# Spectral mixing with a gated FFN on one core: background work queued only when its engine is free, loads counted longer, two phases paced anew

## The chip, the core and the metric

The kernel runs on one core of a Trainium2 chip. The core has five engines with a queue each: TensorE (PE, matrix products), VectorE (DVE), ScalarE (ACT), GpSimd (POOL) and SyncE (SP), which here issues nearly all DMA transfers. Each queue is worked off in the order in which the program was written, and an instruction that waits for a semaphore holds up everything behind it on its engine. The metric is device time in microseconds; lower is better. The kernel before takes 1803.35 us, the median of three runs (1802.31 to 1805.86).

## What is computed

The input `x` is 8192 tokens of 448 features. It is normalised per token, and two things are made of the normalised tokens: a spectral mixing (a Fourier transform over tokens and features, a two-layer block-diagonal MLP on the spectrum, a soft threshold, the inverse transform) and a gated feed-forward net whose result goes through a SiLU. The output is `x + s * g`.

```python
def reference(A_x, A_w1, A_b1, A_w2, A_b2, B_x, B_w_gate, B_w_up, B_w_down):
    def _A_ref(x, w1, b1, w2, b2):            # spectral mixing; 4 blocks of 112 features
        Xf = rfft2(x, axes=(1, 2)); z = Xf.reshape(B, H, Wf, NB, BS)
        hr = zr @ w1[0] - zi @ w1[1] + b1[0];  hi = zi @ w1[0] + zr @ w1[1] + b1[1]
        hr, hi = relu(hr), relu(hi)
        or_ = hr @ w2[0] - hi @ w2[1] + b2[0]; oi_ = hi @ w2[0] + hr @ w2[1] + b2[1]
        or_, oi_ = soft_threshold(or_, 0.01), soft_threshold(oi_, 0.01)
        return irfft2(or_ + 1j * oi_)
    def _B_ref(x, w_gate, w_up, w_down):      # 448 -> 1792 -> 448
        return (_gelu(x @ w_gate) * (x @ w_up)) @ w_down
    xn = _layernorm(A_x)
    s = _A_ref(xn, A_w1, A_b1, A_w2, A_b2)
    g = _silu(_B_ref(xn, B_w_gate, B_w_up, B_w_down))
    return A_x + s * g
```

The block above is shortened; `@` stands for the einsum over one block.

## The kernel before

Products are made in 16-bit pairs: a 32-bit operand is split into a high and a low half, and three products stand for one. The low half is always made by a subtraction (`B.tensor_sub`), the high one by an ACT copy.

**Foreground.** `ffn` runs the feed-forward net in chunks of 512 tokens, in two passes over the 14 blocks of 128 hidden features: pass 0 takes blocks 0 to 7, pass 1 blocks 8 to 13 (`PF`). Each pass has 16 chunks. From chunk 2 on, the gate and up products of a pair of blocks are made in seven products in place of eight (`unit`); its operands are sums and differences of the input's quarters, written to DRAM as `xts` by the background and read back by two transposing DMAs (tiles `xta` and `xtb`). The product with `w_down` is made in the plain way (`down`) until the background has set up the tiles `left` and `right`, and from the next chunk on in seven products too (`down2`).

**Background.** It fills the engines between the foreground's instructions.
- Phase one: `chunk1` takes 512 tokens, normalises them (`stats`, `norm`), makes the operands of the seven products (`factors`, tiles `sf` and `sx`), and does the first stage of the transform (`stage1`: product of `xs` with `m`, then `ysb`). Chunk c enters at `T1 + (c - PL) * DT`. Beside it `weights` prepares the weights: for each far block `gu_loads` loads it into `wst`, `gu_block` finds its largest value (`fm`, then `fx` by way of a small product on PE), scales and splits it, `gu_comb` makes its sums; then `down_weights` and `factors0` do the same for `w_down` (the ACT row `wst<-wst,fd` is their scaling), and `prep_mlp` loads the MLP.
- Phase two: `group` runs the MLP on the spectrum, 16 groups of 4 blocks, spread evenly up to `END2`.
- Phase three: `tiles3` does the last stage of the transform and the gating with what pass 1 of the foreground has stored in `gsp` up to that point. Chunks of pass 1 that begin after phase three is opened are gated directly (`state["direct"]`, `gate_bank`, `gate`), without that round trip.

**The order.** All this is written as coroutines, and `Pace` decides at build time in which order their instructions go into the queues. It keeps a clock per engine from rough costs (`Pace.cost`) and always resumes the coroutine whose time is least; a coroutine that yields gives way. A DMA on SP is counted by `Pace.issue`: 0.5 us of the queue, and a landing 2.2 us plus its size over 240 KB/us after its start. `B` (class `Either`) puts a subtraction on DVE or POOL, whichever ends it first by those clocks. Background instructions go in when their coroutine's turn comes, also when their engine's clock stands further on, and the foreground's next instruction then stands behind them.

On the chip nothing of those clocks is left but the order: an instruction waits for its operands, and what is behind it in its queue waits too. All instructions are recorded from one helper, so each row of the profile says L199, and rows are told apart by their tiles.

Of the kernel before, what the change touches and what calls it, by code (L numbers as in the profile page):

```python
# [13 lines left out]
AF = mybir.ActivationFunctionType  # L14
# [7 lines left out]
NG = 16  # L22
# [17 lines left out]
EPS = 1e-5  # L40
LAM = 0.01
# [7 lines left out]
class Pace:  # L49
# [82 lines left out]
    def issue(self, e, op, out, ins, run):  # L132
        outs, ins, start = self.start(e, out, ins)
        if e == "SP":
# [69 lines left out]
class Either:  # L204
# [5 lines left out]
    def __getattr__(self, op):  # L210
# [7 lines left out]
        return call  # L218

# [154 lines left out]
def afno_geglu_kernel(ctx, tc, x, gu, wd, mlp, b1, b2, c_m, c_mt, c_small, out):  # L374
# [81 lines left out]

    EV = {}
# [46 lines left out]
    def stats(c):  # L504
# [26 lines left out]
    def factors(c, q, xs):  # L531
# [8 lines left out]
        B.tensor_sub(sf[:, 1, :], sf[:, 0, :], xn[:, 0, 0:K1])  # L540
        yield
        B.tensor_sub(sf[:, 3, 0:K2], xn[:, 0, K1:], sf[:, 1, 0:K2])
# [3 lines left out]
        yield  # L546
        S.copy(low[:, 0:K2], sf[:, 3, 0:K2])
        B.tensor_sub(big[:, :, 1, :], sf[:, 0:3, :], big[:, :, 0, :])
        yield
        B.tensor_sub(low[:, K2:K1], sf[:, 3, 128:K2], low[:, 128:K2])  # L550
        B.tensor_sub(low[:, K1:], sf[:, 3, 0:128], low[:, 0:128])
# [39 lines left out]
    def chunk1(c):  # L591
# [5 lines left out]
        for q in range(2):  # L597
            xs = yield from XS.get()
            for a in (2 * q, 2 * q + 1):
                norm(c, a)  # L600
                yield
            xn = EV["x4", c][:, 2 * q:2 * q + 2, :]
            f = pace.spawn(factors(c, q, xs))
            S.copy(xs[:, :, 0, :], xn)
            yield
            B.tensor_sub(xs[:, :, 1, :], xn, xs[:, :, 0, :])
# [27 lines left out]
    T1, DT = 84.0, 42.0  # L634
# [27 lines left out]
    def gu_block(b, to):  # L662

        f0, n = BLK[b]
        for i in range(n):
            yield ev("wl", f0 + i, 0)
            t = EV["wst", f0 + i, 0]
            V.tensor_reduce(fm[:, i, :, b], t[:, 0:8].rearrange("p (i k) f -> p i (k f)", i=2),
# [43 lines left out]
    def gu_split(f, t, d, k):  # L712
        if 0 < f < PF[0][1]:
            for i in range(2):
                w = t[:, 4 * i:4 * i + 4]
                S.activation(w, w, AF.Copy, scale=scale(f, i))
                S.copy(d[:, 0, 4 * i:4 * i + 4], w)
            yield
            for i in range(2):
                B.tensor_sub(d[:, 1, 4 * i:4 * i + 4], t[:, 4 * i:4 * i + 4], d[:, 0, 4 * i:4 * i + 4])  # L720
            yield
            return
        S.activation(d[:, 0, 0:4 - k], t[:, k:4], AF.Copy, scale=scale(f, 0))
# [1495 lines left out]
```

## Time and profile before

| | |
|---|---|
| median of three runs | 1803.35 us (1802.31 to 1805.86) |
| the profiled execution | 1803.61 us, its span 1801.8 us |
| PE busy | 1762.4 us, 98% of the span, 16017 matmuls |
| DVE, ACT, POOL busy | 77%, 57%, 28% |
| mean granted clock of TensorE | 0.996 |
| DMA | 285 MB, 158 GB/s over the span |

The span goes from the first to the last instruction; 1.8 us of the execution lie outside it. A row of a timeline gives the start in us, how long the piece took, the engine, the operation with its tiles (out<-in) and how many instructions are merged; in brackets at its end stands how long the engine had been idle before, and what it had waited for. Rows of windows give each engine's busy time in a stretch of the span, the granted clock of TensorE (PEclk, 1.00 is full speed) and the share of the DMA engines.

### The profile page before, as it was taken

Reading aid. Unit: us, or ns where it says so; the run is one execution under the profiler, and the core shown is the slowest. Engines: PE = TensorE matmul, PEld = TensorE weight load, DVE = VectorE, ACT = ScalarE, POOL = GpSimd, SP = SyncE. Lnnn points to the kernel's source line nnn. Section 1 sums busy time; section 2 is a strip of 40 time slices with the busy share of each in tenths; the row PEclk is TensorE's granted clock in tenths of the full one; section 3 lists DMA queues with packets and bytes.
Section 4 is the critical chain, followed back from the end, with each engine's and each line's share of the span. In section 5 each row is a group of like instructions: output and inputs, shape, how many; then the busy total and the mean of one; then the engine's idle time right before and its main releaser. Section 6 shows DMA issues by size and latency. Waiting matters only on the chain. (4 is left out here: it accounts for less than half of the span.)

```text
span 1801.8 us, 39863 instructions
## 1 busy us (share of the span) xinstructions
PE 1762.4 (98%) x16017; PEld 1457.2 (81%) x16017; DVE 1385.6 (77%) x2518; ACT 1021.1 (57%) x1977; POOL 500.7 (28%) x582
## 2 busy tenths in 40 slices
PE   7999999999999999999999999999999999999998
PEld 3447677776777767898999999999999999888887
DVE  7867587777766668767868878888888887788886
ACT  5736365554554444546767666767767774333333
POOL 3332232231322223212313223233333431221211
PEclk9999999999999999999999999999999999999999
DMA  6454665576647753513335634544344435999991
GB/s 218 159 152 126 172 177 165 170 213 172 192 138 201 199 170 98 162 52 80 77 115 165 184 90 120 120 95 109 87 113 122 114 89 153 302 286 301 315 311 53
DMA packets 353866, 285.35 MB, mean 158 GB/s; under 512 B 235184, under 2 KB 323760, under 8 KB 353680
## 3 DMA queue, kind: packets, MB, share of 16 engines
q1 hardware_dynamic: 353392, 282.24, 55.0%
q8 instruction: 125, 2.05, 0.5%
q10 hardware_dynamic: 288, 0.56, 0.1%
q14 instruction: 61, 0.50, 0.1%
HBM read 128.36 MB, written 105.23 MB: 130 GB/s over the span
## 5 line engine op out<-in xcount | busy, mean ns | idle before, releaser
L199 PEld LDWEIGHTS <-wt 128*128 128x128 f16 x9350 | 909.7, 98 | 170.0 <-issue 14.9
L199 PE MATMUL bx<-xta,wt 128*128 128x256 f16 (+1 forms) x3843 | 475.1, 275 | 0.2 <-ACT th L199 0.2
L199 PEld LDWEIGHTS <-h 128*128 128x128 f16 x2708 | 260.0, 98 | 105.0 <-issue 3.4
L199 PE MATMUL bd<-dw,h 128*128 128x448 f16 (+1 forms) x1704 | 282.8, 317 | 2.5 <-DVE pt L199 0.8
L199 PE MATMUL by<-xtb,wt 128*128 128x256 f16 x2080 | 252.9, 273 | 2.4 <-DVE by L199 2.4
L199 PE MATMUL by<-xta,wt 128*128 128x256 f16 (+1 forms) x1347 | 177.2, 281 | 4.2 <-DVE xta L199 3.1
L199 POOL TENSOR_TENSOR wt<-wt 128x256 f32<-128x256 f32 x78 | 61.3, 786 | 286.2 <-DVE wt L199 270.3
L199 PE MATMUL bx<-xtb,wt 128*128 128x256 f16 x1040 | 130.5, 272 | 1.1 <-DVE v L199 0.7
L199 DVE TENSOR_TENSOR by<-bx,u 128x512 f32<-128x512 f32 x104 | 72.5, 697 | 71.8 <-PE bx L199 64.9
L199 ACT COPY u<-by 128x512 f32<-128x512 f32 x104 | 60.8, 584 | 89.9 <-PE by L199 89.0
L199 POOL TENSOR_TENSOR zs<-t,zs 112x256 f16<-112x256 f32 (+2 forms) x50 | 57.0, 1139 | 159.0 <-ACT zs L199 159.0
L199 ACT ACTIVATE u<-by,fc 128x512 f32<-128x512 f32 (+1 forms) x118 | 73.4, 634 | 46.9 <-PE by L199 46.2
L199 PE MATMUL bd<-dw,wt 128*128 128x224 f16 (+1 forms) x816 | 97.7, 264 | 0.9 <-DVE pt L199 0.6
L199 ACT CAST h<-wt 128x512 f16<-128x512 f32 (+1 forms) x128 | 68.4, 535 | 41.4 <-DVE wt L199 35.7
L199 ACT ACTIVATE th<-bd,fb 128x448 f32<-128x448 f32 x62 | 39.0, 634 | 87.5 <-PE bd L199 72.7
L199 PE MATMUL bf<-w2t,wn 112*128 112x112 f16 x1512 | 84.9, 213 | 0.0
L199 ACT COPY by<-bx 128x512 f32<-128x512 f32 x104 | 59.7, 575 | 42.7 <-PE bx L199 42.3
L199 DVE SCALAR_TENSOR_TENSOR pt<-bd,fb,pt 128x448 f32<-128x448 f32 (+1 forms) x97 | 65.3, 676 | 23.6 <-PE bd L199 22.8
L199 DVE TENSOR_TENSOR v<-bx,u 128x512 f32<-128x512 f32 x104 | 71.2, 685 | 15.8 <-PE bx L199 15.1
L199 PEld LDWEIGHTS <-wn 112*128 112x128 f16 x1512 | 80.6, 98 | 1.2
L199 ACT ACTIVATE gl<-bx,fc 128x512 f32<-128x512 f32 (+1 forms) x70 | 40.5, 600 | 71.0 <-PE bx L199 63.6
L199 DVE SCALAR_TENSOR_TENSOR u<-by,fc,u 128x512 f32<-128x512 f32 (+1 forms) x86 | 55.4, 658 | 25.5 <-PE by L199 13.9
(240 smaller groups left out, 3148.1 us busy)
## 6 DMA issues: line engine op xcount, KB each, us to landing
xts<-sx SPq DMA_DIRECT2D x32, 480.0 KB, 3.0
x<-in_x SPq DMA_DIRECT2D x17, 896.0 KB, 6.5
t<-ysb SPq DMA_DIRECT2D x64, 224.0 KB, 3.3
prt<-th SPq DMA_DIRECT2D x64, 224.0 KB, 2.9
pt<-prt SPq DMA_DIRECT2D x64, 224.0 KB, 3.8
u<-t SPq DMA_DIRECT2D x32, 448.0 KB, 6.2
x<-in_x SPq DMA_DIRECT2D x32, 448.0 KB, 7.0
y<-t SPq DMA_DIRECT2D x30, 448.0 KB, 3.8
```

Source lines behind the costliest of these rows:

```text
L199: return self.pace.issue(self.name, kind, out, ins, lambda: fn(out, *args, **kw))
```

## The change

It has four parts.
1. `CALM`: before a background instruction, its coroutine now waits until its engine's clock is not ahead of the present by more than 0.05 us. For ACT and DVE this is `yield from calm(...)` ahead of the instruction; for subtractions that may go to DVE or POOL it is `B.calm`, which takes the one of the two engines that is free, and if none is, waits for the first that will be. Before 200 us of the order's clock (`QUIET`) nothing of this waits. It is put into `stats`, `factors`, `chunk1`, and the weights' functions (`gu_block`, `gu_split`, `gu_comb`, `factors2`, `down_weights`), not into `stage1`, phase two or phase three.
2. A plain load (DMA into on-chip memory) that starts after 100 us is counted as landing 2.5 us later.
3. Chunks of phase one enter every 38 us in place of 42 (`DT`), so that `END1` moves by 64 us, and the gaps between steps of the far weights are 10 us in place of 20.
4. `END2`, up to which phase two is spread, is 1410 in place of 1450.

```diff
+CALM, QUIET = 0.05, 200.0
...
-                end = max(start + 2.2 + size / 240e3, self.dma + 1.5)
+                end = max(start + 2.2 + size / 240e3, self.dma + 1.5) + (2.5 if outs and start > 100.0 else 0.0)
...
+    def calm(self, op, out, *args):
+        pace = self.pace
+        while True:
+            ends = []
+            for e in self.engines:
+                if pace.free.get(e.name, 0.0) <= pace.now + CALM or pace.now < QUIET:
+                    _, _, start = pace.start(e.name, out, args)
+                    ends.append((start + pace.cost(e.name, op, start, out, args), len(ends), e))
+            if ends:
+                return getattr(min(ends)[2], op)(out, *args)
+            yield min(pace.free[e.name] for e in self.engines)
...
+    def calm(e):
+        while pace.free.get(e, 0.0) > pace.now + CALM and pace.now >= QUIET:
+            yield pace.free[e]
...
+        yield from calm("ACT")
         S.copy(sf[:, 0, K2:], xn[:, 1, K2:K1])
-        B.tensor_add(sf[:, 0, 0:K2], xn[:, 1, 0:K2], xn[:, 1, K1:])
-        B.tensor_sub(sf[:, 2, :], xn[:, 0, 0:K1], xn[:, 1, 0:K1])
+        yield from B.calm("tensor_add", sf[:, 0, 0:K2], xn[:, 1, 0:K2], xn[:, 1, K1:])
+        yield from B.calm("tensor_sub", sf[:, 2, :], xn[:, 0, 0:K1], xn[:, 1, 0:K1])
...
-    T1, DT = 84.0, 42.0
+    T1, DT = 84.0, 38.0
...
             t = EV["wst", f0 + i, 0]
+            yield from calm("DVE")
             V.tensor_reduce(fm[:, i, :, b], t[:, 0:8].rearrange("p (i k) f -> p i (k f)", i=2),
...
+            yield from calm("ACT")
             S.activation(v, v, AF.Copy, scale=fd[:, 2, block(f):block(f) + 1])
...
-    END1, END2, END3 = T1 + NG * DT + 12.0, 1450.0, 1765.0
+    END1, END2, END3 = T1 + NG * DT + 12.0, 1410.0, 1765.0
...
-            yield pace.now + 20.0
+            yield pace.now + 10.0
             pace.spawn(gu_loads(range(BLK[b][0], sum(BLK[b])), 0))
             yield pace.spawn(gu_block(b, 1))
```

Three places show what it does to the order. In these rows a row is one instruction or a run of equal ones (x2), with its tiles and the shape it writes.

The first place is the first pair of far blocks. On SP its two loads are `wst<-in_gu 128x1408`; `xta` and `xtb` are the transposing loads of the foreground's next chunk, the `xts` rows store the background's operands, `t<-ysb` the first stage of the transform. Before:

```order
L199 DMA_TRANSPOSE xta<-xts 128x16x256
L199 DMA t<-ysb 64x1792 x2
L199 DMA_TRANSPOSE xtb<-xts 128x9x256
L199 DMA xts<-sx 128x1920
L199 DMA xts<-xs 128x2x256
L199 DMA xts<-xs 128x2x192
L199 DMA xts<-xs 128x2x64
L199 DMA xts<-xs 128x2x128
L199 DMA t<-ysb 64x1792 x2
L199 DMA wst<-in_gu 128x1408 x2
L199 DMA prt<-th 128x448 x3
```

And on SP of the changed kernel:

```order
L200 DMA t<-ysb 64x1792 x2
L200 DMA xts<-sx 128x1920
L200 DMA xts<-xs 128x2x256
L200 DMA xts<-xs 128x2x192
L200 DMA xts<-xs 128x2x64
L200 DMA xts<-xs 128x2x128
L200 DMA t<-ysb 64x1792 x2
L200 DMA wst<-in_gu 128x1408 x2
L200 DMA_TRANSPOSE xta<-xts 128x16x256
L200 DMA_TRANSPOSE xtb<-xts 128x9x256
```

The two loads stood behind both transposes and now stand ahead of them.

On DVE, at the same place, `fm<-wst` reads those loads, `ysb` is the last piece of the first stage of the transform, the `h`, `gl`, `u`, `v` and `by` rows are the foreground's. Before:

```order
L199 SCALAR_TENSOR_TENSOR gl<-v_1951,fc,gl 128x512
L199 SCALAR_TENSOR_TENSOR ysb<-bf,ysb 128x2x224
L199 TENSOR_TENSOR h<-gl,h 128x2x256
L199 SCALAR_TENSOR_TENSOR ysb<-bf,ysb 128x2x224
L199 TENSOR_REDUCE fm<-wst 128x2 x2
L199 BN_STATS st<-x_1668 128x6
L199 BN_AGGR st<-st 128x2
L199 TENSOR_TENSOR fx<-fm 128x2
```

And on DVE of the changed kernel:

```order
L200 SCALAR_TENSOR_TENSOR ysb<-bf,ysb 128x2x224
L200 TENSOR_TENSOR by<-bx,u_1927 128x512
L200 SCALAR_TENSOR_TENSOR gl<-v_1886,fc,gl 128x512
L200 SCALAR_TENSOR_TENSOR u_1975<-by,fc,u_1975 128x512
L200 TENSOR_TENSOR h<-gl,h 128x2x256
L200 TENSOR_TENSOR v_2001<-bx,u_1927 128x512
L200 TENSOR_TENSOR h<-u_1975,h 128x2x256
L200 SCALAR_TENSOR_TENSOR gl<-v_2001,fc,gl 128x512
L200 BN_STATS st<-x_1563 128x6
L200 BN_AGGR st<-st 128x2
L200 TENSOR_REDUCE fm<-wst 128x2
```

The reduction stood right behind the last `ysb`, and now seven instructions of the foreground and the first statistics stand between them.

The second place is on ACT, at the first `wst<-wst,fd`, which scales the first loaded piece of `w_down`; `xs` is the high half of the background's tokens, from which PE makes the first stage of the transform, and `th` the foreground's output of a chunk. Before:

```order
L199 ACTIVATE th<-bd,fb 128x448 x2
L199 ACTIVATE wst<-wst,fd 128x896
L199 CAST xs<-x_4145 128x2x448
L199 COPY sf<-x_4145 128x64
L199 ACTIVATE th<-bd,fb 128x448
L199 CAST sx<-sf 128x3x256
```

And on ACT of the changed kernel:

```order
L200 ACTIVATE th<-bd,fb 128x448 x2
L200 CAST xs<-x_4344 128x2x448
L200 ACTIVATE th<-bd,fb 128x448
L200 COPY sf<-x_4344 128x64
L200 ACTIVATE wst<-wst,fd 128x896
L200 ACTIVATE ysb<-bf 128x2x224
```

The scaling, which waits for a load, stood ahead of `xs` and now stands behind it.

The third place is on POOL, in a chunk of phase one, from the square roots of its statistics (`st`) on. Before:

```order
L199 TENSOR_TENSOR st<-st 128x4
L199 TENSOR_TENSOR xs<-x_3179,xs 128x2x448
L199 TENSOR_TENSOR sf<-x_3179,sf 128x192
L199 TENSOR_TENSOR sx<-sf,sx 128x3x256
L199 TENSOR_TENSOR h<-gl,h 128x2x256
L199 TENSOR_TENSOR sx<-sf,sx 128x64
L199 TENSOR_TENSOR h<-u_3825,h 128x2x256
```

And on POOL of the changed kernel:

```order
L200 TENSOR_TENSOR st<-st 128x4
L200 TENSOR_TENSOR xs<-x_2525,xs 128x2x448
L200 TENSOR_TENSOR sf<-x_2525 128x192
L200 TENSOR_TENSOR sf<-x_2525 128x256
L200 TENSOR_TENSOR sf<-sf,x_2525 128x256
L200 TENSOR_TENSOR sf<-x_2525,sf 128x192
L200 TENSOR_TENSOR sx<-sf,sx 128x3x256
L200 TENSOR_TENSOR sx<-sf,sx 128x64
L200 TENSOR_TENSOR sx<-sf,sx 128x128
```

POOL did a part of the operands, mixed with subtractions of the foreground's `h`; now it does the whole chain of them in a row. Over the program POOL has 644 instructions where it had 587, and DVE 2463 where it had 2520; ACT has the same number. PE has the same products except for one chunk of pass 1 that is now gated directly (chunks 9 to 14 are gated directly, where 10 to 14 were; the last chunk goes its own way in both): 24 products of 224 columns for 12 of 448. The chunk from which the down product is made in seven products is the same, chunk 12 of pass 0.

More of the change, by code (lines that the diff above doesn't have):

```diff
@@ L599, in chunk1 @@
             for a in (2 * q, 2 * q + 1):
+                yield from calm("DVE")
                 norm(c, a)
@@ L667, in gu_block @@
             t = EV["wst", f0 + i, 0]
+            yield from calm("DVE")
             V.tensor_reduce(fm[:, i, :, b], t[:, 0:8].rearrange("p (i k) f -> p i (k f)", i=2),
@@ L746, in gu_comb @@
             yield ev("spare", f - 2 if f < 6 else f)
+        yield from calm("ACT")
         S.activation(d[:, 0], c, AF.Copy, scale=scale(f, 0))
         yield
+        yield from calm("DVE")
         V.scalar_tensor_tensor(d[:, 1], c, scale(f, 0), d[:, 0], op0=ALU.mult, op1=ALU.subtract)
@@ L757, in factors2 @@
         if block(f) == block(f + 1):
+            yield from calm("ACT")
             S.activation(v, v, AF.Copy, scale=fd[:, 2, block(f):block(f) + 1])
@@ L760, in factors2 @@
             for e in range(2):
+                yield from calm("ACT")
                 S.activation(v[:, e], v[:, e], AF.Copy, scale=fd[:, 2, block(f + e):block(f + e) + 1])
@@ L821, in most @@
             for i in range(n):
+                yield from calm("DVE")
                 V.tensor_reduce(dmx[:, f + i:f + i + 1], v[:, i], axis=AXIS.X, op=ALU.max, apply_absolute_value=True)
```

53 lines of the change are left out of this document (30 added, 23 removed).

## The prediction

> **What bounds the kernel now.** I read the page's engine rows first, then the same by stage, then who waited for whom, then the timeline at the waits that PE ends up with.
>
> ```profile
> span 1801.8 us, 39863 instructions
> PE 1762.4 (98%) x16017; PEld 1457.2 (81%) x16017; DVE 1385.6 (77%) x2518; ACT 1021.1 (57%) x1977; POOL 500.7 (28%) x582
> ...
> 0.00:45.00 45.00, 31.62 (x166) 16.97 (x167) 34.31 (x87) 24.38 (x54) 14.23 (x22) 0.96 0.62 218
> 45.00:90.00 45.00, 41.95 (x213) 19.40 (x212) 39.04 (x83) 32.77 (x61) 13.74 (x14) 1.00 0.50 159
> ...
> 45.00:800.00 755.00, 742.42 (x5528) 536.50 (x5527) 539.97 (x1024) 394.54 (x722) 211.67 (x292) 1.00 0.56 161
> 800.00:1500.00 700.00, 696.67 (x7638) 644.14 (x7637) 568.44 (x1014) 489.79 (x1004) 213.44 (x200) 1.00 0.44 112
> 1500.00:1700.00 200.00, 199.00 (x1838) 177.05 (x1836) 165.13 (x267) 76.50 (x135) 41.70 (x47) 1.00 0.90 280
> 1700.00:1802.00 102.00, 92.67 (x857) 82.53 (x854) 77.78 (x129) 35.85 (x64) 19.66 (x22) 0.98 0.62 195
> ```
>
> The first number after a stretch's length is PE's busy time. PE is the bound in every stage: of 1801.8 us it is idle 39.4. Of these 13.4 lie before 45 us, 3.1 in 45:90 and 9.3 after 1700, most of them filling and draining. What a better order can win is the rest: 12.6 - 3.1 = 9.5 us in 90:800, 3.3 in 800:1500, 1.0 in 1500:1700, together 13.8 us, and what a slowed clock costs beside it.
>
> The waits say where it comes from.
>
> ```profile
> PE bf L199 <- DVE fx L199: 6.3, 2, 3.8
> PE bf L199 <- DVE k L199: 2.5, 4, 1.0
> PE by L199 <- DVE by L199: 2.4, 3, 1.7
> PE bd L199 <- DVE h L199: 0.7, 2, 0.5
> ...
> DVE fm L199 <- DMA wst<-in_gu: 17.8, 4, 14.4
> ...
> ACT wst L199 <- DMA wst<-in_down: 8.2, 3, 3.7
> ```
>
> PE never waits for a transfer itself, but DVE does, for the far blocks' weights, 17.8 us in 4 waits, and ACT, for `w_down`, 8.2 us in 3 (total, times, longest). Both are background instructions, ahead of the foreground's in their queues. The timelines of SP, DVE and PE at the longest of them, with the windows around it:
>
> ```profile
> 196.80 4.12 SPq L199 DMA_TRANSPOSE xtb<-xts  x1
> ...
> 205.29 1.51 SPq L199 DMA_DIRECT2D wst<-in_gu  x2
> ...
> 211.93 1.22 DVE L199 TENSOR_REDUCE fm<-wst 128x2 f32<-128x1024 f32 x1 [14.45 <-DMA wst<-in_gu]
> 214.10 1.22 DVE L199 TENSOR_REDUCE fm<-wst 128x2 f32<-128x1024 f32 x1 [0.95 <-DMA wst<-in_gu]
> ...
> 204.78 5.08 PE L199 MATMUL bd<-dw,h 128*128 128x448 f16 x26
> 209.70 1.47 PE L199 MATMUL bx<-xta,wt 128*128 128x256 f16 x12
> 211.01 1.47 PE L199 MATMUL by<-xta,wt 128*128 128x256 f16 x12
> 216.27 0.59 PE L199 MATMUL bf<-identf,fx 128*2 128x128 f32 x2 [3.79 <-DVE fx L199]
> 216.79 2.74 PE L199 MATMUL bx<-xta,wt 128*128 128x256 f16 x12
> ...
> 215.00:222.00 7.00, 5.73 (x27) 3.76 (x28) 5.06 (x17) 1.41 (x3) 2.06 (x6) 0.52 0.39 155
> ```
>
> The load goes out at 205.29 and lands 6.6 us later, DVE sits 14.45 us on its reduction, and PE has the small product `fx` in its queue and stands still for 3.79 us. After that the granted clock is 0.52 over 7 us: the same twelve products take 2.74 us where they took 1.47. The other places, on ACT, DVE and PE:
>
> ```profile
> 437.59 1.04 ACT L199 ACTIVATE wst<-wst,fd 128x896 f32<-128x896 f32 x1 [3.72 <-DMA wst<-in_down]
> ...
> 439.51 0.35 PE L199 MATMUL bf<-xs,m 128*128 128x448 f16 x1 [0.64 <-ACT xs L199]
> 440.72 0.54 PE L199 MATMUL bf<-xs,m 128*128 128x448 f16 x2 [0.85 <-DVE xs L199]
> ...
> 458.19 1.04 ACT L199 ACTIVATE wst<-wst,fd 128x896 f32<-128x896 f32 x1 [3.60 <-DMA wst<-in_down]
> ...
> 461.64 1.25 PE L199 MATMUL by<-xtb,wt 128*128 128x256 f16 x10 [1.74 <-DVE by L199]
> ...
> 285.78 1.22 DVE L199 TENSOR_REDUCE fm<-wst 128x2 f32<-128x1024 f32 x1 [1.91 <-DMA wst<-in_gu]
> ...
> 287.65 1.25 PE L199 MATMUL by<-xtb,wt 128*128 128x256 f16 x10 [0.31 <-DVE by L199]
> ```
>
> **The change, part by part.** *Loads counted 2.5 us longer.* The old count, 2.2 us plus size over 240 KB/us, gives 5.2 us for a load of 704 KB and 4.1 for 448 KB. What they took, issue to landing:
>
> ```profile
> wst<-in_gu SPq DMA_DIRECT2D x14, 704.0 KB, 6.0
> ...
> wst<-in_down SPq DMA_DIRECT2D x10, 448.0 KB, 5.5
> ```
>
> With 2.5 more the count is 7.7 and 6.6, above both medians, and above the 6.6 of the load at 205.29. So the waits of this kind should shrink by 2.5 us each, and those on the path are of 1.91, 3.72 and 3.60; the 14.45 is a matter of the queue's order.
>
> Term 1, the far block at 212: 3.79 us of idle PE, and half the clock after it. From 215 to 222 a share of 0.48 of the clock is missing, of which the first 1.27 us are idle anyway: (7 - 1.27) x 0.48 = 2.75. Together 6.5 us. Would it be gone? The loads now stand on SP ahead of the two transposes, of which `xtb` alone held SP for 4.12 us. On PE there stand, between the last product of the transform's first stage and `fx`, 64 products of 256 columns and 60 of 448 where there were 24 and 72. By the starts above (209.70 to 211.01 for 12, 204.78 to 209.70 for 26) these take 0.109 and 0.189 us each: 18.3 us now, 16.2 before. Needed are some 3 us for the last `ysb` and the stores ahead of the load (an estimate: twice the 1.51 us that issuing two transfers took), 8.8 until both loads are there (205.29 to 214.10), 1.2 for the second reduction: 13 us of 18. I take all 6.5.
>
> Term 2, the two waits for `w_down`: 0.64 + 0.85 + 1.74 = 3.2 us of PE. At the first, `xs` now stands ahead of the scaling, so that a late load holds up nothing PE waits for; at the second the 3.60 falls to about 1.1, less than the 3.60 - 1.74 = 1.9 that PE had in reserve. All 3.2 gone.
>
> Term 3, at 287: 0.31.
>
> *Background only into a free engine.* An instruction that waits no longer for a turn behind others costs the same engine time, it comes later. The foreground's short waits that are left in 90:800 are 9.5 - 3.8 - 3.2 - 0.3 = 2.2 us, and calm can win at most these. It was put in nowhere after phase one, so the 3.3 and 1.0 us of later stages are touched by the new pace alone. Against it, the order is new everywhere after the first 100 us, and the background is denser. Bounds: all of 2.2 + 3.3 + 1.0 = 6.5 us won, or, on the other side, one more standstill like the one at 212, 6.5 lost. I take 2.2 lost, the short waits of phase one once more; it is nearest to these small ones since the long ones have a cause that goes away.
>
> *The new pace.* No product of PE is gained or lost by it except at one chunk's gating, 24 products of 224 columns for 12 of 448:
>
> ```profile
> L199 PE MATMUL bf<-u,mt 128*128 128x448 f16 x132 | 31.8, 352 | 0.0
> ...
> L199 PE MATMUL bf<-u,mt 128*128 128x224 f16 x120 | 14.6, 259 | 0.0
> ```
>
> 24 x 14.6/120 - 12 x 31.8/132 = 2.92 - 2.89: nothing. The DMA share of 0.90 in 1500:1700 falls with one round trip to DRAM less, but PE is idle only 1.0 us there: nothing. In phase one DVE is busy 540 of 755 us, 72%; 38 us a chunk for 42 make at most 79% of it (an estimate, times 42/38), still under PE.
>
> Sum: 1803.6 - 6.5 - 3.2 - 0.3 + 2.2 = 1795.8 in terms of the profiled execution, which is 0.26 above the median: 1795.5.
>
> **The rivals.** (a) *POOL stretches DVE*: slower. The operands of the seven products now run on POOL in one chain, and POOL has 57 instructions more. The timelines of DVE, POOL and PE show what that can cost:
>
> ```profile
> 1147.09 1.37 DVE L199 TENSOR_TENSOR h<-wt,h 128x256 f16<-128x256 f32 x1
> ...
> 1146.85 1.33 POOL L199 TENSOR_TENSOR h<-wt,h 128x512 f16<-128x512 f32 x1 [0.16 <-ACT h L199]
> ...
> 1148.85 0.49 PE L199 MATMUL bf<-z,w1t 112*112 112x256 f16 x3 [1.01 <-DVE k L199]
> ...
> L199 DVE TENSOR_TENSOR h<-wt,h 128x256 f16<-128x256 f32 x28 | 15.1, 538 | 0.0
> ```
>
> A subtraction of 538 ns on average took 1.37 us while POOL ran one beside it, and PE stood 1.01 us for what came next on DVE. The Trainium skill (SBUF — State Buffer, Who interferes with whom) says that a DVE instruction with two inputs in SBUF and a GpSimd instruction that reads SBUF share one port as an exclusive lock, so that the second blocks fully; by that rule each subtraction moved to POOL is a block for whatever DVE does next with two inputs, and it speaks against this part. The trace agrees at 1147.09. The price: 57 x 1.01 = 58 us if all hit, none if none does. To end above 1807 (the forecast's 8 us and 3.6 more), 12 of the 57 must each cost PE a whole us. The 582 POOL instructions of before go with 2.5 us for `k` and 0.7 for `h`, 3.2 in all, so that 57 more at that rate cost 0.3; but in phase one they now run in chains of seven, beside the foreground's `h`. If it comes, I put it at 1810.
>
> (b) *A load is late again elsewhere*: with 10 us gaps the far blocks come closer together, and one load behind the transposes in SP's queue is enough for a wait of over 3.7 us and the half clock, 6.5 us: 1795.5 + 6.5 = 1802, the same as before. For it: 14.45 us of wait came from one place in a queue. Against it: the 2.5 us.
>
> (c) *Calm takes the short waits too*: all 6.5 us of the better bound: 1803.35 - 10.0 - 6.5 = 1787.
>
> (d) *The change doesn't do what it says*: the weights' end comes later, since calm makes each background step wait, and the down product turns to seven products a chunk later. The order excludes it: it is chunk 12 of pass 0 in both.
>
> **How the numbers follow.** Forecast 0.50, (c) 0.13, (b) 0.20, (a) 0.15, others 0.02. A measurement of this kernel tells about 0.2%, 3.6 us, from no change: faster is below 1799.7, slower above 1807.0. The forecast and (c) are faster but for 0.02 and (b) is so for about a third: 0.67. (b) gives most of no change, with 0.02 of the forecast: 0.17. (a) and the rest of the others: 0.16. The range is 1787 to 1807: it reaches from (c) over the forecast to (b) with a second such wait in part, and leaves (a) out.
>
> **What would show it.** Right: DVE's waits for `wst<-in_gu` fall from 17.8 us to under 5, ACT's for `wst<-in_down` from 8.2 to under 4, no stretch of granted clock near 0.5 after the first 45 us, and PE's idle time in 90:800 from 9.5 us to about 4.5. Rival (a) shows as DVE subtractions of `h` of 256 columns well above 538 ns and as PE waiting for DVE `h`, `by` or `v` by tens; (b) as one PE wait of over 3 us with the clock at half after it. The forecast is wrong if PE's idle time between 90 and 1700 us, 13.8 now, doesn't fall.

## The result, and the profile after

The changed kernel takes 1802.38 us (median of 18 runs, 1799.89 to 1805.37), the kernel before 1804.88 us in 18 runs beside it (1802.31 to 1808.12). The ratio is 0.9984 with a 95% interval of [0.9976, 0.9991]: faster, by 1.6 to 4.3 us (0.0009 and 0.0024 of 1804.88). By the prediction's own bounds (1799.7 and 1807.0) that is no change, and the forecast was 8 us less. The profiled execution took 1800.9 us with a span of 1799.1, against 1803.61 and 1801.8. Below, medians are over all runs of a kernel and ratios over its fast runs alone: one of six runs of e2_end1390 (2294.52 us) and one of ten of e7_without_calm (5938.93 us) were slow.

The page and the windows of the changed kernel, the lines that answer to those of before (a window row: stretch, length, then busy time of PE, PEld, DVE, ACT, POOL with their instructions, granted clock, DMA share, GB/s):

```profile
span 1799.1 us, 39944 instructions
PE 1759.5 (98%) x16029; PEld 1457.2 (81%) x16029; DVE 1374.8 (76%) x2461; ACT 1012.0 (56%) x1977; POOL 521.5 (29%) x639
...
90.00:800.00 710.00, 707.41 (x5501) 526.27 (x5499) 506.30 (x910) 380.94 (x706) 255.20 (x349) 1.00 0.57 165
800.00:1500.00 700.00, 691.76 (x7510) 638.14 (x7508) 559.40 (x999) 464.43 (x966) 182.84 (x190) 1.00 0.45 114
1500.00:1700.00 200.00, 197.26 (x1818) 175.80 (x1816) 163.99 (x264) 73.78 (x130) 41.73 (x48) 1.00 0.92 281
```

A stretch's length less PE's busy time is PE's idle time. In 90:800 it fell from 9.5 us to 2.6, as the forecast wanted; in 800:1500 it rose from 3.3 to 8.2 and in 1500:1700 from 1.0 to 2.7. Over the whole span PE is idle 39.6 us where it was 39.4. Nothing was won in idle time on balance: what is left of the gain is PE's busy time, 1762.4 to 1759.5, which is about the 2.75 us that the prediction worked out for the stretch at half the clock; that stretch is gone.

The place of the long wait, now, in the timelines of SP, DVE and PE and in the window over the time after it:

```profile
193.19 1.30 SPq L200 DMA_DIRECT2D wst<-in_gu  x2
194.59 8.06 SPq L200 DMA_TRANSPOSE xta<-xts  x1
202.75 2.95 SPq L200 DMA_TRANSPOSE xtb<-xts  x1
...
200.17 1.19 DVE L200 TENSOR_REDUCE fm<-wst 128x2 f32<-128x1024 f32 x1
203.48 1.19 DVE L200 TENSOR_REDUCE fm<-wst 128x2 f32<-128x1024 f32 x1
...
186.82 0.73 PE L200 MATMUL bf<-xs,m 128*128 128x448 f16 x3
205.82 0.38 PE L200 MATMUL bf<-identf,fx 128*2 128x128 f32 x2
...
215.00:222.00 7.00, 7.00 (x64) 6.06 (x63) 4.78 (x9) 4.04 (x9) 5.18 (x7) 1.00 0.53 170
```

The loads go out ahead of the transposes, DVE waits for neither (no bracket behind its rows), `fx` comes without idle time on PE, and PE is busy all of 215:222 at full clock.

Where the loss lies, by PE's waits of the changed kernel over the whole span:

```profile
PE bf L200 <- DVE k L200: 5.7, 7, 1.4
...
PE bx L200 <- ACT by L200: 1.9, 1, 1.9
```

The first row (total, times, longest) is phase two's: `k` is the sum of a group step that PE's next product waits for (before: 2.5 us in 4). All 5.7 lie in 800:1500, and with the single wait for ACT's `by` (at 1495 us) they make 7.6 of the 8.2 us there.

One of these steps, in the timelines of ACT, DVE and PE of the changed kernel:

```profile
1326.36 0.37 ACT L200 COPY k<-bf 112x256 f32<-112x256 f32 x1 [1.88 <-PE bf L200]
1326.63 0.58 ACT L200 ACTIVATE vt<-o 128x448 f16<-128x448 f32 x1
...
1327.24 0.63 DVE L200 SCALAR_TENSOR_TENSOR vt<-vt,o 128x448 f16<-128x448 f16 x1 [0.58 <-ACT vt L200]
1327.78 0.42 DVE L200 TENSOR_TENSOR k<-bf,k 112x256 f32<-112x256 f32 x1
...
1328.25 0.54 PE L200 MATMUL bf<-z,w1t 112*112 112x256 f16 x3 [1.41 <-DVE k L200]
```

`vt` belongs to the group one step on. On ACT it stands behind `k`, which waited 1.88 us for PE; on DVE its second half stands ahead of `k`, so that `k` waits for ACT's `vt` first. PE then stands still for 1.41 us. Two neighbouring groups hold each other up here by the order of their instructions; none of the rows shown took longer than 0.63 us.

The wait of 1.89 us at 1495 is another kind. In the timelines of SP, ACT and PE:

```profile
1481.48 10.10 SPq L200 DMA_TRANSPOSE xta<-xts  x1
1491.68 0.58 SPq L200 DMA_DIRECT2D gsp<-th  x1
...
1494.18 0.58 ACT L200 ACTIVATE th<-pt 128x448 f32<-128x448 f32 x1 [4.35 <-DMA gsp<-th]
...
1495.29 1.47 PE L200 MATMUL bx<-xta,wt 128*128 128x256 f16 x12 [1.89 <-ACT by L200]
```

The transpose holds SP for 10.10 us, the store behind it goes out late, ACT's next `th` waits 4.35 us for its buffer, and `by` stands behind `th` on ACT.

### The profile page after: what moved, and what is told of

Same layout as the page of the kernel before. It is cut to its first block, busy times and chain, and to the rows that moved or that the text cites. A ratio compares the mean times of both kernels' runs of the same rounds, so it can differ in the third digit from the quotient of the medians.

```text
span 1799.1 us, 39944 instructions
## 1 busy us (share of the span) xinstructions
PE 1759.5 (98%) x16029; PEld 1457.2 (81%) x16029; DVE 1374.8 (76%) x2461; ACT 1012.0 (56%) x1977; POOL 521.5 (29%) x639
## 5 line engine op out<-in xcount | busy, mean ns | idle before, releaser
L200 POOL TENSOR_TENSOR wt<-wt 128x256 f32<-128x256 f32 x84 | 67.0, 797 | 334.4 <-DVE wt L200 239.5
L200 POOL TENSOR_TENSOR zs<-t,zs 112x256 f16<-112x256 f32 (+1 forms) x40 | 32.2, 804 | 187.1 <-ACT zs L200 160.7
L200 ACT ACTIVATE th<-pt 128x448 f32<-128x448 f32 (+1 forms) x65 | 37.1, 570 | 76.8 <-DVE pt L200 65.9
L200 PEld LDWEIGHTS <-w1t 112*112 112x112 f16 x612 | 68.0, 130 | 9.8 <-DVE k L200 4.0
```

What stands on the lines that cost most here:

```text
L200: return self.pace.issue(self.name, kind, out, ins, lambda: fn(out, *args, **kw))
```

## The experiments

Twelve kernels were run, in three sets of four. The question was twofold: which part wins the 9.7 us of phase one (6.9 of idle time and 2.75 of clock), and what loses the 6.6 of the later stages. Theory A, in its three forms, says that the later loss comes from how phase two's steps fall into each other, and so from the time up to which they are spread (`END2`) rather than from calm, loads or pace. At first it was judged by the places in the order of DVE where `k` stands right behind `vt`, then (A') by those on ACT where `vt` stands right behind `k`, then (A'') by the steps that have both. Theory B, its rival in the first set, puts the loss down to the count of loads.

All results, with PE's idle time by stage worked out from window rows as above. "Half clock" are the stretches between 90 and 1700 us in which the granted clock was 0.5. The last column counts the products of `w_down` made in the plain way (the group `bd<-dw,h` of 448 columns); 96 fewer are one chunk earlier in seven products.

| kernel | ratio [95%] | idle 90:800 | 800:1500 | 1500:1700 | half clock, us | plain products |
|---|---|---|---|---|---|---|
| before | 1 | 9.5 | 3.3 | 1.0 | 6.8 at 214.9 | 1056 |
| after | 0.9984 [0.9976, 0.9991] | 2.6 | 8.2 | 2.7 | none | 1056 |
| e1_end1380 | 0.9953 [0.9941, 0.9965] | 2.6 | 2.7 | 2.4 | none | 1056 |
| e2_end1390 | 0.9943 [0.993, 0.9956] | 2.6 | 1.9 | 1.5 | none | 1056 |
| e3_loads_alone | 1.0038 [1.0026, 1.005] | 11.8 | 1.7 | 3.2 | 3.4 at 217.2, 6.8 at 691.7 | 1056 |
| e4_calm_alone | 1.0052 [1.004, 1.0064] | 9.8 | 6.9 | 3.1 | 3.4 at 217.9 | 1056 |
| e5_without_loads | 0.997 [0.9959, 0.9981] | 7.8 | 2.0 | 2.4 | none | 960 |
| e6_without_pace | 0.9981 [0.9971, 0.9992] | 3.4 | 2.6 | 2.9 | 3.4 at 215.6 | 1152 |
| e7_without_calm | 0.9987 [0.9978, 0.9997] | 9.7 | 2.0 | 1.6 | none | 960 |
| e8_pace_alone | 0.9973 [0.9963, 0.9983] | 8.9 | 3.2 | 2.1 | none | 864 |
| e9_end1450 | 0.9957 [0.9942, 0.9972] | 3.4 | 4.4 | 1.8 | none | 1056 |
| e10_gap0_end1390 | 0.9946 [0.9932, 0.9961] | 3.8 | 3.0 | 3.1 | none | 864 |
| e11_gap4_end1380 | 0.9985 [0.9976, 0.9995] | 5.3 | 6.7 | 1.7 | none | 960 |
| e12_gap4_end1390 | 0.9957 [0.9942, 0.9972] | 5.3 | 2.9 | 1.9 | none | 960 |

### Only the end of phase two: e1 and e2

e1_end1380 is the changed kernel with one number changed:

```diff
-    END1, END2, END3 = T1 + NG * DT + 12.0, 1410.0, 1765.0
+    END1, END2, END3 = T1 + NG * DT + 12.0, 1380.0, 1765.0
```

> The changed kernel with END2 = 1380 in place of 1410, nothing else. In the changed kernel PE idles 8.2 us in 800:1500 (3.3 before), most of it waiting for DVE's `k`. Theory A (place of neighbouring steps): the new spacing of phase two puts the `k` of one step right behind the `vt` of the step before it on DVE (11 times of 68, 1 in the kernel before), so that `k` waits for what `vt` waits for. With END2 = 1380 the order has 2 such pairs: A expects PE idle in 800:1500 back to about 3.5 us and the time 4 to 5 us below the changed kernel's, ratio to the kernel before about 0.996. Theory B (the 2.5 us on loads also reorders phases two and three): END2 doesn't matter, idle stays at 7 to 9 us, ratio 0.998 to 0.999.

Measured: 1794.84 us, ratio 0.9953. e2_end1390 has 1390.0 in the same place.

> The changed kernel with END2 = 1390. The order now has 19 places of 68 with `k` right behind `vt` on DVE. Theory A: PE idle in 800:1500 at least the 8.2 us of the changed kernel, rather 10, waits for `k` above its 5.7 us, ratio 0.999 to 1.001. Theory B: as the changed kernel, 0.998 to 0.999, idle 7 to 9 us.

Measured: 1793.6 us, ratio 0.9943, the fastest of all. The windows of e2_end1390:

```profile
90.00:800.00 710.00, 707.39 (x5509) 526.90 (x5508) 505.44 (x910) 381.73 (x707) 255.99 (x350) 1.00 0.57 165
800.00:1500.00 700.00, 698.15 (x7560) 643.60 (x7558) 565.99 (x1004) 469.55 (x970) 190.28 (x198) 1.00 0.47 122
1500.00:1700.00 200.00, 198.55 (x1846) 178.34 (x1844) 162.02 (x266) 72.20 (x127) 36.95 (x43) 1.00 0.91 268
```

And its row of PE's waits for `k`:

```profile
PE bf L200 <- DVE k L200: 0.9, 3, 0.6
```

Phase one is untouched, to 0.02 us. The 8.2 us of idle time in 800:1500 became 1.9, the wait for `k` went from 5.7 to 0.9, and the one at 1495 is gone too. So, with all else the same, `END2` makes this loss or removes it: that is shown, and theory B is refuted. The measure by which e2 had been expected to be as bad as the changed kernel is refuted too: its order has 19 places on DVE where `k` stands right behind `vt`, against 11 in the changed kernel and 2 in e1, and it is the best.

### Loads alone, calm alone: e3 and e4

e3_loads_alone is the kernel before with part 2:

```diff
-                end = max(start + 2.2 + size / 240e3, self.dma + 1.5)
+                end = max(start + 2.2 + size / 240e3, self.dma + 1.5) + (2.5 if outs and start > 100.0 else 0.0)
```

> The kernel before with part 2 alone (loads after 100 us counted 2.5 us longer). If the load waits are the whole of phase one's gain: DVE's wait for wst<-in_gu falls from 17.8 us to under 5, no half clock after 45 us, PE idle in 90:800 falls from 9.5 to about 3 us, as in the changed kernel (2.6). If calm is needed for it: idle stays above 5. In phase two the order has 19 pairs of `k` behind `vt`: theory A expects idle in 800:1500 of 8 or more, theory B the same, by the loads. Ratio 0.997 to 1.000.

Measured: 1811.19 us, ratio 1.0038, slower than before and than expected. The wait that it was meant to cure is still there, in the timelines of SP and DVE and PE and the windows of e3_loads_alone:

```profile
193.24 4.16 SPq L199 DMA_TRANSPOSE xta<-xts  x1
...
206.68 1.31 SPq L199 DMA_DIRECT2D wst<-in_gu  x2
...
212.26 1.22 DVE L199 TENSOR_REDUCE fm<-wst 128x2 f32<-128x1024 f32 x1 [11.04 <-DMA wst<-in_gu]
...
216.83 2.40 PE L199 MATMUL bx<-xta,wt 128*128 128x256 f16 x12 [2.09 <-ACT by L199]
693.39 2.74 PE L199 MATMUL by<-xta,wt 128*128 128x256 f16 x12 [4.53 <-DVE u L199]
...
217.20:220.60 3.40, 3.40 (x19) 2.34 (x17) 0.76 (x2) 0.09 (x1) 1.84 (x5) 0.50 0.52 202
691.70:698.50 6.80, 5.11 (x25) 3.62 (x26) 6.01 (x26) 2.19 (x4) 3.39 (x3) 0.50 0.20 76
```

The loads go out at 206.68, behind the transposes as before; DVE waits 11.04 us; PE stands still 2.09 us and then runs at half the clock. A standstill of 4.53 us at 689 is new, with a stretch at half the clock behind it. Counting loads as longer does not move these two loads ahead of the transposes. It does work on the loads of `w_down`: ACT's waits for them are 2.8 us here, 8.2 before. Phase two is good: 1.7 us of idle time in 800:1500, where theories A and B both expected 8.

e4_calm_alone is the kernel before with part 1, here at two of its places. It carries one line more that belongs to no part: the loads for direct gating start 20 us after their chunk, where before and after have 10; it acts after 1500 us only.

```diff
+CALM, QUIET = 0.05, 200.0
...
+            yield from calm("DVE")
             V.bn_stats(s6[:, a, :], x4[:, a, :])
...
-        B.tensor_sub(sf[:, 1, :], sf[:, 0, :], xn[:, 0, 0:K1])
+        yield from B.calm("tensor_sub", sf[:, 1, :], sf[:, 0, :], xn[:, 0, 0:K1])
...
-                pace.spawn(load_gate(i), pace.now + 10.0)
+                pace.spawn(load_gate(i), pace.now + 20.0)
```

> The kernel before with part 1 alone (background only into a free engine; loads, DT, gaps and END2 as before). If the load waits come from the count of loads, they stay: DVE's or ACT's waits for wst above 15 us in total and PE idle in 90:800 of 7 to 10 us. If calm takes the short waits: idle falls by up to 2.2 us beside that. In phase two 13 pairs of `k` behind `vt`: theory A expects idle in 800:1500 of 6 to 9 us although no load is counted longer, theory B 3 to 4 us. Ratio by A 1.000 to 1.003, by B 0.998 to 1.000.

Measured: 1813.29 us, ratio 1.0052, slower than before and than expected. Its waits:

```profile
DVE fm L200 <- DMA wst<-in_gu: 16.4, 3, 12.8
...
PE bf L200 <- DVE fx L200: 6.4, 3, 3.5
PE bf L200 <- DVE k L200: 5.7, 7, 1.4
```

The 12.8 us wait, PE's standstill of 3.5 us and the half clock stay, and phase two has the changed kernel's loss to the digit. It is the same loss: PE's timeline between 800 and 1500 us has the same seven standstills at the same distances (to 0.3 us), 11 us earlier. The first and the largest of them, in e4_calm_alone:

```profile
1022.77 0.54 PE L200 MATMUL bf<-z,w1t 112*112 112x256 f16 x3 [0.90 <-DVE k L200]
...
1317.59 0.53 PE L200 MATMUL bf<-z,w1t 112*112 112x256 f16 x3 [1.41 <-DVE k L200]
```

And in the changed kernel the first of them, beside the one at 1328.25 above:

```profile
1033.73 0.54 PE L200 MATMUL bf<-z,w1t 112*112 112x256 f16 x3 [0.89 <-DVE k L200]
```

The two programs share neither pace nor `END2` (42 and 1450 here, 38 and 1410 there). Compared word for word, though, ACT's orders between the first and the last `k` share one unbroken stretch of 695 of 1047 instructions, DVE's one of 681 of 1075.

### One part out: e5, e6, e7, and the pace alone: e8

e5_without_loads is the changed kernel with the old count:

```diff
-                end = max(start + 2.2 + size / 240e3, self.dma + 1.5) + (2.5 if outs and start > 100.0 else 0.0)
+                end = max(start + 2.2 + size / 240e3, self.dma + 1.5)
```

> The changed kernel without part 2 (loads counted as in the kernel before); calm, pace and END2 = 1410 as changed. What cures phase one (PE idle in 90:800: 9.5 us before, 2.6 changed; loads alone 11.8, calm alone 9.8)? Theory P (pace): the shorter gaps put the first far loads ahead of the transposes on SP, here too; idle in 90:800 is 2 to 4 us with or without the count of loads. Theory L (loads): the count is needed beside it; DVE and ACT wait for wst above 8 us again and PE idle is 6 us or more. On ACT the order has 8 places where `vt` stands right behind `k` (16 changed, 8 before): theory A' (that order on ACT decides phase two, not `k` behind `vt` on DVE) expects idle in 800:1500 of 2 to 4 us.

Measured: 1799.08 us, ratio 0.997. The idle time of phase one is back to 7.8 us, as theory L expected, but without the standstill at 212, as theory P did.

e6_without_pace is the changed kernel with the old chunks and the old gaps (and the one gap for direct gating at 20, as in e4):

```diff
-    T1, DT = 84.0, 38.0
+    T1, DT = 84.0, 42.0
...
-            yield pace.now + 10.0
+            yield pace.now + 20.0
...
-        yield pace.spawn(factors0(10.0))
+        yield pace.spawn(factors0(20.0))
```

> The changed kernel with DT = 42 and gaps of 20 us as before; loads, calm and END2 = 1410 as changed. The first far loads stand behind the transposes on SP again. Theory P: DVE's wait for wst<-in_gu is above 10 us, one wait of PE over 2 us with the half clock after it, idle in 90:800 of 7 us or more. Theory L: idle in 90:800 of 2 to 4 us. On ACT 5 places with `vt` behind `k`: A' expects idle in 800:1500 of 2 to 3.5 us.

Measured: 1799.82 us, ratio 0.9981. Phase two is good (2.6 us of idle time). Phase one has its standstill again, as theory P expected, but with 3.4 us of idle time in all, as theory L did. SP's and PE's timelines and the window behind the standstill:

```profile
191.24 4.37 SPq L200 DMA_TRANSPOSE xta<-xts  x1
...
205.28 2.05 SPq L200 DMA_DIRECT2D wst<-in_gu  x2
...
215.45 2.60 PE L200 MATMUL bx<-xta,wt 128*128 128x256 f16 x12 [2.71 <-ACT by L200]
...
215.60:219.00 3.40, 3.40 (x18) 2.35 (x17) 0.84 (x3) 0.31 (x1) 0.00 (x0) 0.50 0.59 233
```

e7_without_calm is the changed kernel without part 1: each `yield from calm(...)` is gone and each `B.calm` is the plain call again, as in the kernel before.

```diff
-            yield from calm("DVE")
             V.bn_stats(s6[:, a, :], x4[:, a, :])
...
-        yield from B.calm("tensor_sub", sf[:, 1, :], sf[:, 0, :], xn[:, 0, 0:K1])
+        B.tensor_sub(sf[:, 1, :], sf[:, 0, :], xn[:, 0, 0:K1])
```

> The changed kernel without part 1 (the kernel before with loads counted longer, DT = 38, gaps of 10, END2 = 1410). If calm takes short waits of the foreground: idle in 90:800 is 2 us or more above the changed kernel's 2.6. If calm is of no use: 2 to 3 us. On ACT 9 places with `vt` behind `k`: A' expects idle in 800:1500 of 2 to 4 us.

Measured: 1801.68 us, ratio 0.9987. No standstill at 212 and no half clock after 90 us, but 9.7 us of short waits in phase one.

e8_pace_alone is the kernel before with part 3:

```diff
-    T1, DT = 84.0, 42.0
+    T1, DT = 84.0, 38.0
...
-            yield pace.now + 20.0
+            yield pace.now + 10.0
...
-        yield pace.spawn(factors0(20.0))
+        yield pace.spawn(factors0(10.0))
```

> The kernel before with DT = 38 and gaps of 10 alone, END2 = 1450 and loads as before. Theory P: no standstill at the first far block, DVE's wait for wst<-in_gu under 8 us, idle in 90:800 of 3 to 5 us with the waits of ACT for wst<-in_down still there. Theory L: 7 us or more. On ACT 14 places with `vt` behind `k`: A' expects idle in 800:1500 of 6 to 8 us.

Measured: 1799.49 us, ratio 0.9973. Phase one keeps 8.9 us of idle time, as theory L expected. Its SP and DVE at the place of the standstill:

```profile
192.92 1.30 SPq L199 DMA_DIRECT2D wst<-in_gu  x2
194.32 8.00 SPq L199 DMA_TRANSPOSE xta<-xts  x1
...
198.48 1.22 DVE L199 TENSOR_REDUCE fm<-wst 128x2 f32<-128x1024 f32 x1 [3.75 <-DMA wst<-in_gu]
```

Four things follow. First, the pace is what puts the loads ahead of the transposes: every kernel with it (the changed one, e5, e7, e8) has no standstill at 212 and no half clock behind it, every kernel without it (before, e3, e4, e6) has both. Second, the short waits of phase one go only with calm and loads together. PE's idle time in 90:800 is 9.5 us with nothing, 11.8 with loads, 9.8 with calm, 8.9 with pace, 7.8 with calm and pace, 9.7 with loads and pace, 3.4 with calm and loads and 2.6 with all three. Either of the two without the other is worth 1.1 us at most (calm, with the pace) and costs up to 2.3 (loads, alone). Third, the pace alone, ratio 0.9973 [0.9963, 0.9983], is not told apart from the whole change. Over the span its PE is busy 1756.8 us, where the changed kernel's is busy 1759.5:

```profile
PE 1756.8 (98%) x16175; PEld 1470.8 (82%) x16175; DVE 1414.7 (79%) x2576; ACT 1027.9 (57%) x2001; POOL 477.2 (27%) x586
```

The pace alone ends the weights two chunks earlier (864 plain products for 1056); calm takes one of them back (e5), loads take one back (e7 has 960 too), and with both the old chunk is reached again. What a chunk is worth is not settled. The plain products and all the groups of seven products that take their place (`bd` and `by` from `dw`, `wt` or `right` with `h` or `left`) add up to 437.7 us in the changed kernel, 436.9 in e5 and 437.5 in e8, where groups that overlap count twice; by PE's busy time over the span, e8 is 2.7 us below the changed kernel for two chunks. Fourth, the loss of phase two is not tied to the value of `END2`: with the 1410 of the changed kernel, taking out the loads, the pace or the calm leaves 2.0, 2.6 and 2.0 us of idle time in 800:1500, and calm alone has the loss with 1450. It belongs to the order that the four parts make together.

For A', e8 was a miss: its order has 14 places on ACT with `vt` right behind `k`, close to the changed kernel's 16, and 3.2 us of idle time in 800:1500, where 6 to 8 were expected. What sets the changed kernel and e4 apart from it is two steps that have both pairs, on ACT and on DVE; e2, e7 and e8 have one such step and the others none. That is A''.

### A'' put to the test: e9 to e12

e9_end1450 is the changed kernel with part 4 undone (1450.0 for 1410.0 in the line of e1).

> The changed kernel with part 4 undone (END2 = 1450). Theory A'' (phase two loses where the same step has both `vt` right behind `k` on ACT and `k` right behind `vt` on DVE; two such steps in the changed kernel, two with calm alone, none or one in all other kernels run so far): none here, so idle of PE in 800:1500 of 2 to 3.5 us in place of 8.2, and the time about 5 us below the changed kernel's, ratio 0.994 to 0.997. If it is END2 itself, an earlier end of phase two being better (1380 and 1390 were better than 1410): idle of 8 us or more and a ratio of 0.999 or above.

Measured: 1797.76 us, ratio 0.9957. The 4.4 us in 800:1500 are more than the 2 to 3.5 expected: 1.9 are the wait for ACT's `by` behind a transpose that held SP, as at 1495, so that the 1410 is not what brings this wait; the wait for `k` is 0.7. So the changed kernel without its fourth part is faster than with it: the intervals [0.9942, 0.9972] and [0.9976, 0.9991] do not touch.

The next two belong together. e10_gap0_end1390 has the gaps of the far weights at nothing and `END2` at 1390, to get the two lost chunks back; e11_gap4_end1380 has gaps of 4 us and 1380, an order of phase two with two steps that have both pairs, though 1380 had been good in e1; e12_gap4_end1390 is e11 with 1390. The edit of e11 (e10: 0.0 and 1390.0, e12: 4.0 and 1390.0):

```diff
-            yield pace.now + 10.0
+            yield pace.now + 4.0
...
-        yield pace.spawn(factors0(10.0))
+        yield pace.spawn(factors0(4.0))
...
-                pace.spawn(load_gate(i), pace.now + 10.0)
+                pace.spawn(load_gate(i), pace.now + 4.0)
...
-    END1, END2, END3 = T1 + NG * DT + 12.0, 1410.0, 1765.0
+    END1, END2, END3 = T1 + NG * DT + 12.0, 1380.0, 1765.0
```

> The changed kernel with gaps of 0 us in place of 10 in the far weights and END2 = 1390. The down product turns to seven products two chunks earlier (864 products of 448 columns from `h` where the changed kernel has 1056). Theory W (a chunk in seven products saves 168 x 0.096 against 96 x 0.189 us, 2.0 us, and the kernel is bound by PE): 4 us less than e2_end1390, ratio about 0.992. If the denser background costs as much as that: 0.994 or above, with idle of PE in 90:800 above 6 us.

> Gaps of 4 us and END2 = 1380. Two steps of phase two have `vt` behind `k` on ACT and `k` behind `vt` on DVE (19 places on ACT): A'' expects idle of PE in 800:1500 of 6.5 to 9 us, and ratio 0.996 to 0.998 although END2 is that of e1_end1380 and the seven products begin one chunk earlier. If END2 = 1380 is good in itself: idle under 3.5 us, ratio 0.994.

> Gaps of 4 us and END2 = 1390: the same kernel as e11_gap4_end1380 up to phase two, but no step of that kind (7 places on ACT). A'' expects idle of PE in 800:1500 of 1.5 to 3.5 us, about 5 us below e11_gap4_end1380, ratio 0.992 to 0.994.

Measured: e10 1795.82 us, ratio 0.9946; e11 1801.64, 0.9985; e12 1797.54, 0.9957. e11 has 6.7 us of idle time in 800:1500 and e12, which differs from it only in `END2`, 2.9. PE's waits and the first and largest standstill of e11:

```profile
PE bf L200 <- DVE k L200: 5.7, 7, 1.4
...
1041.19 0.54 PE L200 MATMUL bf<-z,w1t 112*112 112x256 f16 x3 [0.89 <-DVE k L200]
...
1335.73 0.54 PE L200 MATMUL bf<-z,w1t 112*112 112x256 f16 x3 [1.41 <-DVE k L200]
```

It is the same seven standstills a third time, 7.5 us later than in the changed kernel, in a program whose `END2` is 30 us earlier. Here too one unbroken stretch of the order is that of the changed kernel, 582 instructions of ACT and 595 of DVE; with e12 the longest such stretch is 15 and 11. So the loss goes with an order, not with a moment: that is shown. A'' foretold which of the last four kernels would lose, but as a mechanism it reaches less far. In the traces of the changed kernel, e4 and e11 the two steps that have both pairs are those of the first and the largest of the seven standstills, 0.89 + 1.41 = 2.3 of the 5.7 us; the other five, 3.4 us, come at steps with one pair or none. And in e2, e7 and e8 PE does not wait for `k` at the one step that has both. In e8's timelines of DVE and PE, PE's next product of that kind has no idle time ahead of it:

```profile
1358.19 0.42 DVE L199 TENSOR_TENSOR k<-bf,k 112x256 f32<-112x256 f32 x1
...
1359.11 0.49 PE L199 MATMUL bf<-z,w1t 112*112 112x256 f16 x3
```

What else in the shared stretch makes PE wait stays open: no run changed the pairs alone.

e10 did get its two chunks (864 plain products) and is no faster than e2: its idle time is higher by 1.2 us in 90:800, 1.1 in 800:1500 and 1.6 in 1500:1700, together 3.9. The saving in products that was expected is not seen: over the span PE is busy 1759.4 us where it is 1758.4 in e2, and a stretch of 3.4 us at half the clock at 50 us, which this execution of e10 has and that of e2 has not, accounts for at most 1.7 us, so that by this pair 0.7 us were saved at most. The ratios of e10, e11 and e12 were expected lower than they came.

The best version is e2_end1390, 1793.6 us. It beats the kernel before by 0.44 to 0.70% and the changed kernel by about 0.4% (0.9943 against 0.9984). e1, e9, e10 and e12 are not told apart from it by their intervals.

## Why the prediction was right or wrong

**The standstill at 212: right, by the wrong part.** All of the 6.5 us are gone. That it is gone took some luck: the working put 13 us of work into the 18.3 between the transform's last product and PE's need of `fx`. In the trace PE's part is 187.55 to 205.82, 18.3 as worked out, but the second reduction ends at 204.67, 17.1 us after the start of that stretch; 1.1 were left and not 5. The loads went out 5.6 us into it, where 3 had been put, and were reduced 11.5 us later, where 10 had been put. And the gain stood under the heading of the loads counted longer, and loads alone (e3) leave the standstill; the pace removes it (e8).

**The waits for `w_down`, and the one at 287: right.** The changed kernel has no wait of ACT's `wst` for `in_down` left, and none of PE for `by` in 90:800. The count of the loads does most of it and calm the rest: 8.2 us of ACT's waits before, 2.8 with loads alone, 9.2 with calm alone, none with the two (e6).

**The 2.2 us lost to the new order: the step that failed.** Two things were wrong in it. It was put into phase one, where nothing was lost: 2.6 us of idle time, and the forecast's sum leaves 9.5 - 3.8 - 3.2 - 0.3 + 2.2 = 4.4. And the sentence that the later stages "are touched by the new pace alone", with nothing to pay there, was where the kernel lost 6.6 us: 4.9 in 800:1500 and 1.7 in 1500:1700. The paragraph on the pace weighs the gating, the DMA share and DVE's load; the fourth part of the change, `END2`, has no term at all, nor has what the new order does to phase two, though the 8.2 us of idle time in 800:1500 fall to between 2.0 and 4.4 when any one of the four parts is taken out (e5, e6, e7, e9). The "one more standstill, 6.5 lost" that stood as the outer bound for a new order has the size of what came, by chance: it came as short waits, none above 1.9 us. The 1.7 in 1500:1700 was traced to no part: there every kernel but the one before has 1.5 to 3.2 us of idle time. With 6.6 in place of the 2.2 the terms give 1803.6 - 10.0 + 6.6 = 1800.2; the profiled execution took 1800.9.

**The pace costs PE nothing: true of the whole, not of the part.** "No product of PE is gained or lost by it" holds for the four parts together: pace alone makes two more chunks in seven products, and calm and loads give both back. By the two profiles that cost no more than the 2.7 us of busy time between e8 and the changed kernel. Rival (d) looked at the start chunk, found chunk 12 in both, and did not ask why three parts that move it left it there.

**Gating and DMA.** The 24 products for 12 cost nothing, as said. The DMA share in 1500:1700 did not fall (0.90 to 0.92).

**Rival (a), POOL stretches DVE: refuted.** DVE's and POOL's subtractions of `h` in the groups of the changed kernel:

```profile
L200 DVE TENSOR_TENSOR h<-wt,h 128x256 f16<-128x256 f32 x17 | 8.6, 504 | 0.0
...
L200 POOL TENSOR_TENSOR h<-wt,h 128x256 f16<-128x256 f32 x31 | 25.7, 829 | 0.1
```

DVE's take 504 ns on average where they took 538; POOL's went from 725 to 829. POOL is busy 521.5 us where it was 500.7, and PE's waits for DVE's `h` fell from 0.7 to 0.3 us. The Trainium skill (SBUF — State Buffer, Who interferes with whom), on which this rival drew, says that such a pair blocks each other fully and that the first to issue keeps the port. In these rows the averages fit a block that falls on POOL more often than on DVE, and POOL has time; which of the two blocked at a given place was not measured.

**Rival (b)** gave the right time, 1802, by a mechanism that did not come: no load was late again, and no standstill after 100 us reaches 2 us. **Rival (c)** was half right: the short waits of phase one did go, all but 2.6 us.

**The signs named.** DVE's and ACT's waits for the loads fell below the stated bounds, no half clock came between 45 and 1700 us, and idle time in 90:800 went below the stated 4.5. The sign for a wrong forecast came too: PE's idle time between 90 and 1700 us is 2.59 + 8.24 + 2.74 = 13.6, against 13.8.

## What to carry to other kernels

Where an order written at build time decides, give every part of a change a term in every stage, also where it was "put in nowhere": a number that only shifts when a stage ends can move more time than the instructions that were rewritten. Read a bundle by taking one part out at a time, since in phase one two parts that are worth nothing or less alone take away most of the short waits together, and one part alone is not told apart from all four. After a change upstream, try the constants downstream again: two other values of one number (1380 and 1390 for 1410) were worth 5.6 and 7.4 us (0.0031 and 0.0041 of 1802.38).

## What the hardware showed that was not expected

**A short standstill of PE can bring the half clock, or not.** Behind 4.53 us of idle PE (e3) and 3.79 (before) the clock was 0.5 for 6.8 us; behind 2.09 (e3), 2.71 (e6) and 3.49 (e4) for 3.4; behind 1.89 (the changed kernel at 1495) not at all. The two stretches of 6.8 us began while PE still stood (at 214.9 and 691.7, PE going on at 216.27 and 693.39), those of 3.4 within 0.4 us after it had gone on. The same standstill of 2.48 us, which every kernel has at 46 us, is followed by the half clock in eight of the fourteen profiled executions. PE's timeline and the window, of e5_without_loads and then of the changed kernel:

```profile
49.73 0.59 PE L200 MATMUL bf<-identf,fx 128*2 128x128 f32 x2 [2.48 <-DVE fx L200]
...
49.50:52.90 3.40, 3.17 (x10) 1.09 (x11) 3.40 (x8) 3.33 (x7) 1.26 (x3) 0.50 0.47 113
```

```profile
49.04 0.38 PE L200 MATMUL bf<-identf,fx 128*2 128x128 f32 x2 [2.48 <-DVE fx L200]
...
49.50:52.90 3.40, 3.40 (x23) 1.72 (x21) 3.40 (x8) 3.34 (x7) 1.43 (x2) 1.00 0.66 169
```

The two programs differ only in the count of loads after 100 us, so at 2.48 us something other than the length of the standstill decides. The Trainium skill (TensorE: Matmul & The Clock Gate, What's actually happening) says that the clock is set by free-running windows of some 3.4 us. The stretches of 3.4 and 6.8 us agree with that, and so does it that the same standstill is punished or not, by where in a window it falls. By the same place the clock falls after an idle window of some 3.4 us; here 2.09 us sufficed.

**A transpose holds its queue twice as long behind loads.** The first `xta` after 190 us held SP for 4.16, 4.23 and 4.37 us where the two loads of 704 KB stood behind it (e3, e4, e6), and for 8.06, 7.57, 7.82 and 8.00 where they stood just ahead of it (the changed kernel, e5, e7, e8). The longest in the changed kernel is 10.10 us, behind other transfers. Moving a load ahead of a transpose therefore took some 3.6 us more of the queue (7.86 on average against 4.25); here PE had the time.
